# Spread tokens in SBUF instead of PSUM: a long convolution and a mixture of 4096 one-row experts on one core

## The chip, the cores and the metric

The kernel runs on one core of one Trainium2 chip. The metric is the device time of one execution in microseconds (us); lower is better. Five engines work side by side, each through its own queue of instructions in a fixed order, and wait for one another by semaphores: PE (matmul; PEld is its weight load), DVE (elementwise), ACT (activation functions and copies), POOL (here: it makes the descriptors of the indirect gathers and does some small arithmetic) and SP (issues the plain DMAs).

## The reference

Everything works on 2048 tokens of 448 channels. One half (A) is a long causal convolution per channel, the other (B) a layer of product-key experts:

```python
xn = _layernorm(x)
# A: short conv on k, times v, long conv by FFT, gate
kv = k_shift * v;  y = irfft(rfft(kv_pad) * rfft(k_pad))[:S] + kv * ssm_D;  A = xn * y
# B: 16 heads, two sets of 64 keys, best 2 of the 64x64 pairs
q1, q2 = halves of einsum("nd,dhc->nhc", xn, w_q)
s1, s2 = q1 @ k1.T, q2 @ k2.T          # two best of each, then two best sums
g = softmax(top_s);  ue, ve = u[top_e], v[top_e]
act = gelu(einsum("nd,nhkd->nhk", xn, ue))
B = einsum("nhk,nhk,nhkd->nd", g, act, ve)
out = x + A + B
```

B needs 2048 x 16 x 2 = 65536 gathered rows, each 448 numbers of `u` and 448 of `v` (3584 bytes): 235 MB, the bulk of the kernel's traffic.

## The kernel before

Tokens lie on the 128 partitions, 16 tiles T of them in `XA`. Scores are found with matmuls against weights folded from `w_q` and the keys, the best experts with MAX8 and FIND_INDEX8 on DVE; `place` turns the expert numbers into `idx` and the softmax weights into `gat`, spread so that one gather fetches, for 32 tokens, four experts each.

The expert work of a tile is cut into `NB` = 8 batches (128 in all, b = 8T + j). One batch is:

- **gather**: four indirect DMAs on POOL's queue (L586), each 128 rows of `u` and `v` side by side into one of the `ring`'s slots. The ring holds `RING` = 5 batches, so that the gathers of batch b + 5 wait until batch b has been used. A gather also waits for the landing of the sixth gather before it, and for a matmul on PE that the plan puts `LEAD` us ahead of it.
- **prod** (L619): one DVE multiplication of the four `u` slots (128 x 1792 numbers) with `xs`, the tile's tokens spread so that partition p holds the token of the row gathered there. Before, `xs` lies in PSUM (four of the eight banks), where `spread` (L607) writes it with four matmuls per tile.
- **sum** and **gelu** (L625, L627): four ACT copies with accumulation, then one small activation.
- **co** and **coef** (L633, L632): two small multiplications that make the matmul's weights `cc` from gelu, `gat` and a constant; on POOL up to batch 103, on DVE from `LATE` = 104 on.
- **val** (L638): four matmuls from `cc` and the `v` slots into `pv`, which gathers the tile's result in its own bank; `fold` (L673) takes it out.

The convolution (A) runs in between as matrix products in two parts: `conv_in` (L703 to L724), `spectrum` (L767 to L796), `inverse` (L814 to L839), `conv_out` (L858 to L881). In its elementwise steps DVE multiplies and adds pieces of `S`, which is in SBUF (L703, L704, L707 to L709, L795, L796), or a PSUM bank with SBUF (L788, L839).

All other matrix products share the remaining PSUM banks, three before: a product takes a slot with `acq`, and the instruction that reads it out last gives it back with `rel`.

The order of all this on each engine is made by a planner (`Plan.solve`): it goes through time, starts on each engine the ready operation with the smallest key, and knows durations, hops between engines and free banks. `RANK` shifts the keys of each group of operations along the kernel. The planner also fills planned gaps on PE between `val`s with idle matmuls (L1094), which write columns of `pv` that nobody reads.

Of the kernel before, what the change touches and what calls it, by code (L numbers as in the profile page):

```python
# [15 lines left out]
ALU = mybir.AluOpType  # L16
# [2 lines left out]
S, D, H, E = 2048, 448, 16, 64  # L19
NT = S // P  # L20
NB = 8
RING = 5


N = 2 * S
# [69 lines left out]
class Plan:  # L95
# [122 lines left out]
        "in1": (388.1, 396.9), "sp1": (396.9, 561.6), "out1": (561.6, 586.6)}  # L218
DMA_RATE = 0.421
OUTSTANDING = 6  # L220
LEAD = 2.0
RANK = {
# [6 lines left out]
    "SPlate@out1": (-46.5, -46.5, -46.5, -57.0), "SPwq": (0.0, 0.0, 45.5, 0.0), "SPx": (6.0, 6.0, 19.5, 22.0), "bad": (178.0, 100.0, 62.0, 46.5),  # L229
    "co": (-1740.0, 1197.0, -1227.0, -3082.0), "coef": (-33.5, -40.5, -46.0, 6.0), "ds": (22.0, -93.0, -157.5, -36.0),  # L230
    "es": (79.5, 106.0, 108.5, 109.0), "fin@out0": (-413.0, -296.5, -286.5, 40.5), "fin@out1": (0.5, -32.0, -27.5, -27.5),
    "flag": (-22.5, -47.5, -14.0, -53.0), "fold": (50.0, 36.5, 0.0, 0.0), "gat": (13.0, 13.0, 13.0, 9.0), "gate@out1": (6.5, 14.5, -60.5, -123.0),
    "gateG@out0": (83.0, -13.0, 54.5, 64.0), "gateG@out1": (-81.0, -64.5, -137.5, -144.0), "gather": (2080.5, 2339.0, 2195.5, 3324.0),
    "gelu": (164.5, 57.0, 133.0, 285.5), "hh@sp0": (8.0, -21.0, -25.0, -24.5), "hh@sp1": (123.5, 413.0, 124.0, 164.0),
    "idx": (-94.5, -44.0, 35.5, -83.0), "join": (-75.5, -75.5, -75.0, -66.0), "kv@in0": (-829.5, -476.5, -686.5, -690.5),
    "kv@in1": (85.0, 90.5, 112.5, 143.0), "landing": (36.0, 242.5, 1246.5, -266.5), "late@out1": (87.0, -40.5, -164.0, -260.0),
    "lateD@out1": (344.5, 342.0, 247.0, 196.0), "mi": (-280.5, -150.0, 455.5, 455.5), "mx": (-7077.5, -8642.5, -7977.0, -6331.5),
    "newton": (67.5, 142.0, 224.5, 283.5), "pk": (-14.5, -10.0, -32.0, -8.0), "place": (-628.5, -829.0, -301.5, -212.5),
# [6 lines left out]
    "stats": (1206.5, 960.0, 979.0, 837.5), "store": (43.0, 28.0, 12.5, 7.0), "storeD": (23.5, 22.0, 74.0, 52.5),  # L245
# [3 lines left out]
    "tw@sp1": (-23.5, -160.0, -53.5, -133.5), "val": (87.5, -236.5, 21.0, -42.0), "whi": (495.0, 545.0, 210.5, 67.0),  # L249
# [4 lines left out]
}  # L254
LATE = 104
DLAND = 1.2
# [17 lines left out]
def one_pass(ctx, tc, x, wq, kk, uv, kvh, cst1, cst2, fq, out, flag):  # L274
# [22 lines left out]
    ds = ap.tile([P, P], F32, name="ds")  # L297
    nw = ap.tile([P, 64], F32, name="nw")

    xs = pp.tile([P, 4, 512], F32, name="xs")  # L300
    pv = pp.tile([P, 512], F32, name="pv")
    bank = [pp.tile([P, 512], F32, name=f"bank{i}") for i in range(3)]

    ident, i4, rmask = c1[:, 0:P], c1[:, P:2 * P], c1[:, 2 * P:2 * P + 4]
    off8, one = c1[:, 2 * P + 4:2 * P + 12], c1[:, 2 * P + 12:]
# [35 lines left out]
    ws = [S1[:, D * i:D * i + D] for i in range(2)]  # L341

    pl = Plan()
    pl.pool("bank", 3)
    op = pl.op

    def load(dst, src, mb, w, key, nb=0.0, r=(), name=""):
# [46 lines left out]
    def tb(b):  # L394
        return T0 + PACE * min(b, TURN) + PACE2 * max(b - TURN, 0)
# [205 lines left out]
            landed.append(d)  # L601

    def spread(T):
        def f():
            for r in range(4):
                rs = slice(32 * r, 32 * r + 32)
                nc.tensor.matmul(xs[:, r, :D], i4[rs, :], XA[rs, T, :], start=True, stop=True, tile_position=(32 * r, 0))  # L607
        op("PE", 1.1, f, r=[("x", T), "c1"], w=["xs"], key=tb(NB * T) - 6.0, name="spread")

    def batch(T, j):  # L610
        b = NB * T + j
        k = tb(b)
        U = ring[:, b % RING, :, :D]
        aw = sm[:, 4 * (b % 4):4 * (b % 4) + 4]
        ge = sm[:, 16 + 4 * (b % 4):20 + 4 * (b % 4)]
        co = sm[:, 32 + 4 * (b % 4):36 + 4 * (b % 4)]
        u = [("U", b % RING, r) for r in range(4)]
        m = 4
        op("DVE", dve(m * D), lambda: nc.vector.tensor_mul(U[:, :m, :], U[:, :m, :], xs[:, :m, :D]), r=["xs"], w=u[:m], key=k, name="prod")  # L619
        for r in range(m, 4):  # L620
            op("DVE", 0.78, lambda r=r: nc.vector.scalar_tensor_tensor(U[:, r, :], xs[:, r, :D], 1.0, U[:, r, :], op0=ALU.mult, op1=ALU.mult,
                                                                      accum_out=aw[:, r:r + 1]),
               r=["xs"], w=[u[r], ("aw", b % 4, r)], key=k, name="dot")
        for r in range(m):
            op("ACT", 0.575, lambda r=r: nc.scalar.activation(U[:, r, :], U[:, r, :], AF.Copy, accum_out=aw[:, r:r + 1]),  # L625
               w=[u[r], ("aw", b % 4, r)], key=k, name="sum")
        op("ACT", 0.2, lambda: nc.scalar.activation(ge, aw, AF.Gelu_apprx_tanh), r=[("aw", b % 4, r) for r in range(4)], w=[("ge", b % 4)], key=k, name="gelu")  # L627

        ve, en, d0, d1 = (nc.vector, "DVE", 0.17, 0.3) if b >= LATE else (nc.gpsimd, "POOL", 0.22, 0.41)

        def coef():
            last_val(ve.tensor_mul(cc[b % 3], co[:, :, None].broadcast_to([P, 4, 32]), rep[:, None, :].broadcast_to([P, 4, 32])).ins, b - 3)  # L632
        op(en, d0, lambda: ve.tensor_mul(co, ge, gat[:, T % 8, :, j]), r=[("ge", b % 4), ("gat", T % 8, j // 2)], w=[("co", b % 4)], key=k - 40.0, name="co")  # L633
        op(en, d1, coef, r=[("co", b % 4), "c1"], w=[("cc", b % 3)], key=k - 40.0, name="coef")

        def val():
            for r in range(4):
                v = nc.tensor.matmul(pv[32 * r:32 * r + 32, :D], cc[b % 3][:, r, :], ring[:, b % RING, r, D:],  # L638
                                     start=(j == 0), stop=(j == NB - 1), tile_position=(0, 32 * r)).ins
                tc.declare_no_dep(v, group=GROUP + "s", reason="the coefficients come from all four gathered slots")  # L640
                if r < 3:
                    tc.add_to_no_dep_group(GROUP, v)
            vins[b] = v.name
        v = op("PE", 1.0, val, r=[("cc", b % 3)] + ([("pv", j - 1)] if j else []) + ([("pv", n) for n in more(T)] if j == NB - 1 else []), w=[("V", b % RING, r) for r in range(4)] + [("pv", j)] + (["pv"] if j == 0 else []), key=k, name="val")
        v.slot = j
# [511 lines left out]
```

## Time and profile before

| | |
|---|---|
| median of 3 runs | 918.38 us (917.74 to 920.84) |
| the profiled execution | 909.46 us, its span 907.5 us, granted clock 0.907 |
| PE / PEld busy | 750.7 / 474.3 us |
| DVE / ACT / POOL busy | 672.4 / 568.3 / 590.5 us |
| HBM read and written | 272.29 and 6.08 MB, 307 GB/s over the span |
| first and last gather start | 40.6 and 876.5 us |

Busy time is what an engine's instructions took. Waiting, issuing of DMAs and the pause between two gathers on POOL are not in it. In a row of groups stand the line, the engine, the operation, what it writes and reads, the count, then busy us and mean ns of one, then the idle time of that engine just before and what ended it.

### The profile page before, as it was taken

The numbers are of one execution on the slowest core, as the hardware profiler recorded it, in microseconds if no ns is written. First come the engines' busy times: TensorE is split into PE (matmuls) and PEld (weight loads), VectorE is DVE, ScalarE is ACT, GpSimd is POOL, SyncE is SP. The second block draws the span as 40 slices with busy tenths as digits, with TensorE's granted clock in tenths as the row PEclk, the third lists the DMA queues.
The fourth block names the chain that finished last, engine by engine and source line by source line (L and its number), as shares of the span: only waits on it lengthen the run. The fifth ranks groups of instructions, "written<-read, shape, count | busy, mean of one in ns | idle before, by whom it ended". The sixth has DMA issues, their size and how long they took to land.

```text
span 907.5 us, 15150 instructions
## 1 busy us (share of the span) xinstructions
PE 750.7 (83%) x4696; PEld 474.3 (52%) x4696; DVE 672.4 (74%) x1570; ACT 568.3 (63%) x1874; POOL 590.5 (65%) x740
## 2 busy tenths in 40 slices
PE   6978988898888888889798887788598897859776
PEld 2436655655565555556465555465343443436554
DVE  3667988797878877777878867658798897863553
ACT  2698664566556765566664576536698896864552
POOL 0157487877777766767677677747778776665640
PEclk9999999997999988989899889888989998986887
DMA  9998699888889898889899889988989999899975
GB/s 370 368 384 293 202 315 309 296 284 303 306 312 328 306 313 273 299 308 324 284 307 328 306 292 373 361 287 295 324 300 324 335 301 327 313 328 338 304 259 141
DMA packets 62586, 279.47 MB, mean 308 GB/s; under 512 B 14112, under 2 KB 23584, under 8 KB 62240
## 3 DMA queue, kind: packets, MB, share of 16 engines
q0 software_dynamic: 40960, 234.91, 74.4%
q1 hardware_dynamic: 21536, 43.49, 13.5%
q8 instruction: 39, 0.64, 0.3%
q14 instruction: 51, 0.42, 0.1%
HBM read 272.29 MB, written 6.08 MB: 307 GB/s over the span
## 4 chain that ended last, share of the span: by engine, by line
PE 42%; DVE 15%; issue 12%; POOL 10%; ACT 9%; DMA 8%; another core or an unknown queue 3%; DVEq 0%; POOLq 0%; SPq 0%; ACTq 0%
PE pv L638 9%; POOL ring L586 8%; DVE ring L619 4%; ACT ring L625 4%; DVE SC L486 4%; DMA ring<-in_uv_dram,idx 4%; PE bank L771 3%; PE bank L477 3%; PE bank L720 3%; PE bank L865 3%; PE pv L1094 3%; PE bank L478 3%; PE bank L479 3%; PE bank L814 2%
## 5 line engine op out<-in xcount | busy, mean ns | idle before, releaser
L586 POOL DMA_INDIRECT ring<-in_uv_dram,idx x512 | 505.4, 987 | 253.6 <-issue 91.9
L625 ACT ACTIVATE ring<-ring 128x448 f32<-128x448 f32 x512 | 288.3, 566 | 42.3 <-DVE ring L619 28.1
L619 DVE TENSOR_TENSOR ring<-ring,xs 128x1792 f32<-128x1792 f32 x128 | 256.8, 2013 | 36.1 <-DMA ring<-in_uv_dram,idx 28.0
L638 PE MATMUL pv<-ring,cc 128*32 128x448 f32 x1024 | 141.9, 622 | 49.1 <-POOL cc L632 24.6
L486 DVE MAX8 SC<-bank 128x8 f32<-128x64 f32 x512 | 118.4, 232 | 43.9 <-PE bank L481 12.2
L1094 PEld LDWEIGHTS pv<-c 128*128 128x128 f32 x596 | 82.1, 204 | 28.8 <-issue 27.8
L625 ACT ACTIVATION_READ_ACCUMULATOR ring<-ring 128x1 f32 x512 | 97.0, 189 | 0.0
L720 PE MATMUL bank<-c,S 128*64 128x132 f32 x896 | 71.6, 305 | 27.1 <-issue 7.5
L1094 PE MATMUL pv<-c 128*128 128x64 f32 x596 | 87.3, 287 | 2.5 <-issue 2.5
L477 PE MATMUL bank<-WR,xh 128*128 128x512 f32 x192 | 84.6, 441 | 4.9 <-issue 2.8
L720 PEld LDWEIGHTS bank<-c,S 128*64 128x64 f32 x896 | 56.2, 150 | 50.8 <-issue 22.6
L478 PE MATMUL bank<-WR,xh 128*128 128x512 f32 x192 | 77.0, 401 | 0.0
L479 PE MATMUL bank<-WR,xl 128*128 128x512 f32 x192 | 76.6, 399 | 0.0
L638 PEld LDWEIGHTS pv<-ring,cc 128*32 128x32 f32 x1024 | 21.6, 114 | 91.7 <-issue 37.2
L771 PE MATMUL bank<-x1b,S 128*128 128x336 f32 x132 | 53.0, 520 | 12.1 <-issue 4.6
L788 DVE TENSOR_TENSOR S<-bank,S 128x224 f32<-128x224 f32 (+1 forms) x66 | 40.6, 618 | 26.0 <-ACT S L782 12.1
L724 ACT ACTIVATE x1b<-bank 128x264 f32<-128x264 f32 x84 | 31.1, 387 | 45.5 <-PE bank L720 36.8
L703 DVE TENSOR_TENSOR S<-S 128x1024 f32<-128x1024 f32 x28 | 34.2, 1221 | 30.0 <-PE bank L720 11.4
L477 PEld LDWEIGHTS bank<-WR,xh 128*128 128x128 f32 x192 | 37.9, 197 | 29.6 <-issue 9.1
L493 DVE FIND_INDEX8 SC<-SC,bank 128x8 uint32<-128x256 f32 x128 | 52.5, 423 | 0.0
L632 POOL TENSOR_TENSOR cc<-sm,c 128x128 f32<-128x128 f32 x104 | 46.0, 443 | 2.1
L782 ACT ACTIVATE S<-bank 64x112 f32<-64x112 f32 x132 | 33.9, 256 | 18.2 <-PE bank L767 6.5
(142 smaller groups left out, 1102.8 us busy)
## 6 DMA issues: line engine op xcount, KB each, us to landing
R<-in_wq_dram SPq DMA_DIRECT2D x16, 896.0 KB
S<-in_kvh_dram SPq DMA_DIRECT2D x28, 400.0 KB
ring<-in_uv_dram,idx POOLq DMA_INDIRECT x512
S<-in_fq_dram SPq DMA_DIRECT2D x32, 128.0 KB
XA<-in_x_dram SPq DMA_DIRECT2D x2, 1344.0 KB
out_dram<-fo SPq DMA_DIRECT2D x12, 224.0 KB
x1b<-out_dram SPq DMA_DIRECT2D x9, 224.0 KB
out_dram<-XA SPq DMA_DIRECT2D x2, 840.0 KB
```

The source lines that it names most:

```text
L477: nc.tensor.matmul(o, xh[:, c, :], wh[:, c, ns], start=(c == 0), stop=False)
L478: nc.tensor.matmul(o, xh[:, c, :], wl[:, c, ns], start=False, stop=False)
L479: nc.tensor.matmul(o, xl[:, c, :], wh[:, c, ns], start=False, stop=False)
L486: nc.vector.max(mx[:, 8 * n + j, :] if safe else m2[:, m, 2 * j:2 * j + 8], bank[s.i][:, 64 * j:64 * j + 64])
L493: nc.vector.max_index(m4i[:, 2 * m + g, :], m2[:, m, 8 * g:8 * g + 8], bank[s.i][:, 256 * g:256 * g + 256])
L586: g = nc.gpsimd.indirect_dma_start(dst, None, uv, bass.IndirectOffsetOnAxis(ap=idx[:, T % 8, r, j:j + 1], axis=0)).ins
L619: op("DVE", dve(m * D), lambda: nc.vector.tensor_mul(U[:, :m, :], U[:, :m, :], xs[:, :m, :D]), r=["xs"], w=u[:m], key=k, name="prod")
L625: op("ACT", 0.575, lambda r=r: nc.scalar.activation(U[:, r, :], U[:, r, :], AF.Copy, accum_out=aw[:, r:r + 1]), w=[u[r], ("aw", b % 4, r)] ...
L638: v = nc.tensor.matmul(pv[32 * r:32 * r + 32, :D], cc[b % 3][:, r, :], ring[:, b % RING, r, D:], start=(j == 0), stop=(j == NB - 1), tile_ ...
L720: nc.tensor.matmul(o[64 * i:64 * i + 64, w * j:w * j + w], src, f1[:, i, :], start=True, stop=True, tile_position=(0, 64 * i))
L771: op("PE", 0.95 * n / 448 + 0.05, lambda t=t, sl=sl: nc.tensor.matmul(bank[sl.i][:, :n], fm, x1[p][:, :, q, t, :], start=True, stop=True), ...
L1094: nc.tensor.matmul(pv[:, D:], ident, c1[:, P:P + 512 - D], start=False, stop=False)
```

## The change

`xs` becomes an SBUF tile with two buffers, one for even and one for odd tiles. A spread matmul now writes an ordinary bank, and an ACT copy brings it to SBUF; there are four of each per tile. The product reads both operands from SBUF. The four PSUM banks that `xs` had go to the shared pool: seven instead of three. The SBUF that the two buffers take (14336 bytes per partition) is what the ring gives up: four batches instead of five. `LEAD` goes from 2.0 to 1.0, and all numbers in `RANK` are new, with seven points along the kernel instead of four.

```diff
-RING = 5
+RING = 4
...
-LEAD = 2.0
+LEAD = 1.0
 RANK = {
-    "DMAc1": (-1.0, 0.0, 8.0, 64.5), "DMAc2": (43.5, 4.0, 37.0, 128.5), ...
+    "DMAc1": (-28.0, -15.5, -74.0, -74.5, -52.5, -48.0, -73.5), ...
...
-    xs = pp.tile([P, 4, 512], F32, name="xs")
+    xs = ap.tile([P, 2, 4, D], F32, name="xs")
     pv = pp.tile([P, 512], F32, name="pv")
-    bank = [pp.tile([P, 512], F32, name=f"bank{i}") for i in range(3)]
+    bank = [pp.tile([P, 512], F32, name=f"bank{i}") for i in range(7)]
...
-    pl.pool("bank", 3)
+    pl.pool("bank", 7)
...
     def spread(T):
-        def f():
-            for r in range(4):
+        for r in range(4):
+            sl = Slot()
+
+            def f(r=r, sl=sl):
                 rs = slice(32 * r, 32 * r + 32)
-                nc.tensor.matmul(xs[:, r, :D], i4[rs, :], XA[rs, T, :], start=True, stop=True, tile_position=(32 * r, 0))
-        op("PE", 1.1, f, r=[("x", T), "c1"], w=["xs"], key=tb(NB * T) - 6.0, name="spread")
+                nc.tensor.matmul(bank[sl.i][:, :D], i4[rs, :], XA[rs, T, :], start=True, stop=True, tile_position=(32 * r, 0))
+            k = tb(NB * T) - 12.0
+            op("PE", 0.27, f, r=[("x", T), "c1"], w=[("sp", r)], key=k, acq=("bank", sl), name="spread")
+            op("ACT", 0.54, lambda r=r, sl=sl: nc.scalar.activation(xs[:, T % 2, r, :], bank[sl.i][:, :D], AF.Copy), r=[("sp", r)], w=[("xs", T % 2, r)],
+               key=k, rel=("bank", sl), name="xs")
...
-        op("DVE", dve(m * D), lambda: nc.vector.tensor_mul(U[:, :m, :], U[:, :m, :], xs[:, :m, :D]), r=["xs"], w=u[:m], key=k, name="prod")
+        op("DVE", dve(m * D), lambda: nc.vector.tensor_mul(U[:, :m, :], U[:, :m, :], xs[:, T % 2, :m, :]), r=[("xs", T % 2, r) for r in range(4)], w=u[:m], key=k, name="prod")
```

Three places show what the new order does. In these rows `bank0` and so on are PSUM slots, `cc0` to `cc2` the coefficients in turn, L477 to L481 (L494 to L498 after) the score products, L767 and L814 (L832 after) convolution products.

PE at the spread of tile 6, before: one write into `xs`, after the `val` of batch 46 (the tile's first batch is 48).

```order
L480 MATMUL bank2_88<-WR_93,xh_95 128x512
L481 MATMUL bank2_88<-WR_93,xl_96 128x512
L638 MATMUL pv_85<-ring_66,cc1_75 32x448 x4
L607 MATMUL xs_84<-XA_65,c1_67 128x448 x4
L767 MATMUL bank0_86<-R1_94,S1_72 128x224
L638 MATMUL pv_85<-ring_66,cc2_76 32x448 x4
L767 MATMUL bank1_87<-R1_94,S1_72 128x224
```

PE at the spread of tile 6 after: two of its four matmuls, each into a bank of its own, after the `val` of batch 30.

```order
L656 MATMUL pv_85<-ring_66,cc2_76 32x448 x4
L832 MATMUL bank3_89<-S1_72,c2_68 128x112 x4
L656 MATMUL pv_85<-ring_66,cc0_74 32x448 x4
L832 MATMUL bank3_89<-S1_72,c2_68 128x112 x4
L626 MATMUL bank1_87<-XA_65,c1_67 128x448
L626 MATMUL bank5_91<-XA_65,c1_67 128x448
L494 MATMUL bank6_92<-WR_97,xh_99 128x512
```

The spread moved two tiles ahead of its use; it no longer holds one fixed place in PSUM until the tile is done, but each part needs a free slot and an ACT copy that frees it.

ACT around batch 47, the last of tile 5, before: the sums (L625) and the gelu (L627) of one batch after another, with convolution copies (L782) and the fold (L673).

```order
L627 ACTIVATE sm_77<-sm_77 128x4
L625 ACTIVATE ring_66,sm_77<-ring_66 128x448 x4
L627 ACTIVATE sm_77<-sm_77 128x4
L782 ACTIVATE S1_72<-bank0_86 64x112 x4
L673 ACTIVATE fo_69<-pv_85,mv_78 128x448
```

ACT at the same place after: the four copies into `xs` (L629) for tile 7 come in one piece behind the sums (L643) of batch 46 and ahead of those of batch 47.

```order
L643 ACTIVATE ring_66,sm_77<-ring_66 128x448 x4
L645 ACTIVATE sm_77<-sm_77 128x4
L853 ACTIVATE R1_98<-bank4_90,c2_68 128x28x4 x2
L629 ACTIVATE xs_84<-bank6_92 128x448
L629 ACTIVATE xs_84<-bank1_87 128x448
L629 ACTIVATE xs_84<-bank5_91 128x448
L629 ACTIVATE xs_84<-bank2_88 128x448
L643 ACTIVATE ring_66,sm_77<-ring_66 128x448 x4
L645 ACTIVATE sm_77<-sm_77 128x4
```

ACT has four more instructions per tile; they stand nine batches ahead of the first product that reads them, batch 56.

POOL around batch 40, before: gathers (L586) with co (L633) and coef (L632) woven in; when the coef of batch 40 (the L632 that writes `cc1`) comes, 18 gathers beyond the 160 of the batches up to 39 have been issued.

```order
L586 DMA ring_66<-in_uv_dram,idx_70 128x896 x7
L633 TENSOR_TENSOR sm_77<-sm_77,gat_71 128x4
L586 DMA ring_66<-in_uv_dram,idx_70 128x896
L632 TENSOR_TENSOR cc1_75<-sm_77,c1_67 128x128
L586 DMA ring_66<-in_uv_dram,idx_70 128x896
L633 TENSOR_TENSOR sm_77<-sm_77,gat_71 128x4
L586 DMA ring_66<-in_uv_dram,idx_70 128x896
L632 TENSOR_TENSOR cc2_76<-sm_77,c1_67 128x128
```

POOL around batch 40 after: the same instructions, L603, L651 and L650, with 12 gathers beyond the 160 at the coef of batch 40 (`cc1`).

```order
L603 DMA ring_66<-in_uv_dram,idx_70 128x896 x5
L651 TENSOR_TENSOR sm_77<-sm_77,gat_71 128x4
L650 TENSOR_TENSOR cc0_74<-sm_77,c1_67 128x128
L651 TENSOR_TENSOR sm_77<-sm_77,gat_71 128x4
L650 TENSOR_TENSOR cc1_75<-sm_77,c1_67 128x128
L603 DMA ring_66<-in_uv_dram,idx_70 128x896 x2
L651 TENSOR_TENSOR sm_77<-sm_77,gat_71 128x4
L603 DMA ring_66<-in_uv_dram,idx_70 128x896
L650 TENSOR_TENSOR cc2_76<-sm_77,c1_67 128x128
```

POOL's work is the same 512 gathers, 104 co and 104 coef; its gathers run up to one batch and a half less ahead of the coefficients.

More of the change, by code (lines that the diff above doesn't have):

```diff
@@ L220 @@
 OUTSTANDING = 6
-LEAD = 2.0
+LEAD = 1.0
 RANK = {
[6 rows of a table removed]
[L229 to L238, printed above, removed]
[6 rows of a table removed]
-    "stats": (1206.5, 960.0, 979.0, 837.5), "store": (43.0, 28.0, 12.5, 7.0), "storeD": (23.5, 22.0, 74.0, 52.5),
[3 rows of a table removed]
-    "tw@sp1": (-23.5, -160.0, -53.5, -133.5), "val": (87.5, -236.5, 21.0, -42.0), "whi": (495.0, 545.0, 210.5, 67.0),
[4 rows of a table removed]
[10 rows of a table added]
+    "SPx": (15.0, 15.0, 15.0, 15.0, 11.0, 15.0, 15.0), "bad": (38.5, 47.0, 35.5, 26.0, 69.5, 47.5, 29.0),
[3 rows of a table added]
+    "flag": (6.0, -5.0, -5.0, -5.0, -5.0, -18.0, -5.0), "fold": (-1.0, -18.5, -44.0, -58.5, 8.5, 14.0, 7.5),
[20 rows of a table added]
+    "stats": (1100.5, 1019.5, 922.5, 949.5, 972.5, 929.5, 942.5), "store": (-4.5, -12.0, -9.0, -1.5, -3.0, -4.0, -4.0),
[5 rows of a table added]
+    "val": (96.5, -364.5, -547.5, -311.5, 22.5, -332.5, 206.5), "whi": (43.0, 58.5, 20.5, 3.5, -28.5, -19.5, -19.5),
[6 rows of a table added]
 }
@@ L618, in batch @@
         m = 4
[L619 to L623, printed above, removed]
+        op("DVE", dve(m * D), lambda: nc.vector.tensor_mul(U[:, :m, :], U[:, :m, :], xs[:, T % 2, :m, :]), r=[("xs", T % 2, r) for r in range(4)], w=u[:m], key=k, name="prod")
         for r in range(m):
```

63 rows, old and new, of the table RANK are left out of this document.

## The prediction

> **What bounds the kernel now.** I read the page's head, then the stretches, then POOL's waits, its timeline against DVE's, and the groups.
>
> ```profile
> span 907.5 us, 15150 instructions
> PE 750.7 (83%) x4696; PEld 474.3 (52%) x4696; DVE 672.4 (74%) x1570; ACT 568.3 (63%) x1874; POOL 590.5 (65%) x740
> ...
> 0.00:77.00 77.00, 60.61 (x324) 31.24 (x328) 43.49 (x156) 49.18 (x156) 21.96 (x32) 0.96 0.94 367
> 77.00:877.00 800.00, 670.63 (x4266) 428.41 (x4258) 616.82 (x1397) 510.93 (x1696) 568.04 (x709) 0.91 0.89 308
> 877.00:907.50 30.50, 19.49 (x110) 14.63 (x110) 12.10 (x19) 8.16 (x24) 0.47 (x1) 0.69 0.51 147
> ```
>
> The page's 65% for POOL hides its pauses. In the timeline a gather begins 0.30 us after a gather and 0.16 us after a small multiplication:
>
> ```profile
> 636.26 0.96 POOL L586 DMA_INDIRECT ring<-in_uv_dram,idx  x1
> 637.24 0.41 POOL L632 TENSOR_TENSOR cc<-sm,c 128x128 f32<-128x128 f32 x1
> 637.81 1.90 POOL L586 DMA_INDIRECT ring<-in_uv_dram,idx  x1 [0.16 <-issue]
> 640.02 0.95 POOL L586 DMA_INDIRECT ring<-in_uv_dram,idx  x1 [0.30 <-PE bank L720]
> ...
> 77.00:877.00 800.00, 484.81 (x491) 0.91 0.89 308
> ...
> 77.00:877.00 800.00, 6.07 (x21) 45.18 (x102) 0.91 0.89 308
> ```
>
> The last two rows are the stretch for the gathers (L586) and for coef (L632: DVE's, then POOL's): 491 gathers, 102 coefs on POOL, and a co (L633) to each. So about 204 gathers follow a multiplication and 287 a gather: 204 x 0.16 + 287 x 0.30 = 119 us of pauses. POOL's time is then 568 + 119 = 687 of 800 us, 86%: it is as full as PE (671 us, which includes idle matmuls). 113 us are real waiting:
>
> ```profile
> POOL ring L586 <- issue: 86.4, 330, 1.2
> POOL sm L633 <- ACT sm L627: 23.4, 19, 3.3
> POOL ring L586 <- PE bank L720: 15.9, 21, 4.0
> POOL ring L586 <- PE pv L638: 13.9, 16, 2.0
> POOL ring L586 <- remote: 11.7, 13, 2.0
> ```
>
> The first row is the pauses; the rest, and a tail of smaller rows, are spread thin. No engine has a large reserve that the others could lean on, and POOL has 14%.
>
> **The product's second operand.** This term decides. The gather that took 1.90 us above, where 0.95 is usual, began inside a DVE instruction that reads two SBUF tensors:
>
> ```profile
> 637.64 1.22 DVE L703 TENSOR_TENSOR S<-S 128x1024 f32<-128x1024 f32 x1
> ...
> L586 POOL DMA_INDIRECT ring<-in_uv_dram,idx x512: 940/948/1978, 40.6 to 876.5; - x171
> ...
> 106.83 1.81 POOL L586 DMA_INDIRECT ring<-in_uv_dram,idx  x1 [0.30 <-issue]
> ...
> 106.60 1.22 DVE L703 TENSOR_TENSOR S<-S 128x1024 f32<-128x1024 f32 x1
> ```
>
> L703 ended at 638.86, the gather at 639.71: 0.85 later. At 106.83 L703 ended at 107.82 and the gather at 108.64: 0.82 later. All 13 gathers that began inside L703 with more than 0.25 us of it left did this (these two are the first and the last). A gather thus needs about 0.13 us at its start that it cannot have while such an instruction runs; then it goes on. The product of today does not do that:
>
> ```profile
> 57.40 0.94 POOL L586 DMA_INDIRECT ring<-in_uv_dram,idx  x1 [6.04 <-ACT gat L562]
> 876.52 0.95 POOL L586 DMA_INDIRECT ring<-in_uv_dram,idx  x1 [0.30 <-issue]
> ...
> 55.99 2.02 DVE L619 TENSOR_TENSOR ring<-ring,xs 128x1792 f32<-128x1792 f32 x1
> 876.28 2.02 DVE L619 TENSOR_TENSOR ring<-ring,xs 128x1792 f32<-128x1792 f32 x1 [3.10 <-DMA ring<-in_uv_dram,idx]
> ```
>
> These are the first and the last of 163 gathers that began inside a product; the longest took 1.0 us. The one difference that fits is that `xs` is in PSUM. Co and coef behave alike: coef on POOL spans 398/409/1457 ns, and its long ones (such as the first row here) began inside S<-S instructions.
>
> ```profile
> 625.15 1.42 POOL L632 TENSOR_TENSOR cc<-sm,c 128x128 f32<-128x128 f32 x1
> ...
> L632 POOL TENSOR_TENSOR cc<-sm,c x104: 398/409/1457, 64.2 to 744.0; 128x128 f32<-128x128 f32 x104
> ```
>
> After the change all 128 products are of the holding kind, and each is longer than L703.
>
> [...]
>
> **The parts of the change and their cost.**
>
> *Hold by the product.* I laid the two timelines over one another: in 121 of 128 products some gather, co or coef starts. Counting only the first start in each product, since POOL is in order, and the product's remaining time less 0.13 us for a gather, the sum is 160 us, 1.25 per product. A check from spacing: a product lasts 2.01 us, and a busy POOL starts something about every 0.95 + 0.30 us, so the first start comes 0.6 us into it and waits 2.01 - 0.6 - 0.1 = 1.3. Best case, each product begins right behind a gather's start: 2.01 - 1.25 - 0.13 = 0.63, or 81 us. Worst case, a start right behind each product's: 2.01 - 0.13, or 241 us. I take 155 for the 123 products of the middle stretch.
>
> *The product itself* costs about the same:
>
> ```profile
> L619 DVE TENSOR_TENSOR ring<-ring,xs x128: 1998/2012/2022, 56.0 to 882.4; 128x1792 f32<-128x1792 f32 x128
> L703 DVE TENSOR_TENSOR S<-S x28: 1205/1224/1226, 81.3 to 642.8; 128x1024 f32<-128x1024 f32 x28
> L707 DVE TENSOR_TENSOR S<-S x21: 673/691/694, 491.8 to 644.2; 128x512 f32<-128x512 f32 x21
> ```
>
> From 512 to 1024 numbers takes 533 ns, 1.04 each, with 158 fixed; 1792 give 2.02 us, 11 ns more than now and 1.4 us over 128. DVE has room for it. [...]
>
> *ACT copies.* 64 copies, priced by a copy of that shape:
>
> ```profile
> L418 ACT ACTIVATE S<-bank x16: 519/530/544, 13.5 to 66.4; 128x448 f32<-128x448 f32 x16
> ```
>
> That is 34 us on an engine with 511 of 800 us busy, nine batches ahead of use: nothing on the path. If that cover failed, each tile would pay 4 x 0.53 = 2.1 us behind the sums, 34 us in all. The wait that goes, a product for the spread, was 3.3 us in 3 cases; next late there is the landing of the gathers (28.0 us in 18 cases).
>
> *Seven banks.* What PE or its weight loads waited for an eviction by ACT or DVE:
>
> ```profile
> PE bank L767 <- ACT ring L625: 8.2, 3, 4.1
> PE bank L865 <- ACT S L860: 6.4, 5, 3.0
> PEld bank L767 <- ACT ring L625: 12.1, 6, 4.3
> PEld bank L865 <- ACT S L860: 10.8, 7, 3.8
> PEld bank L720 <- ACT ring L625: 10.6, 15, 1.9
> PEld bank L720 <- ACT x1b L724: 8.6, 6, 2.9
> ```
>
> These are 57 us, smaller rows bring perhaps as much; part of it is data that was late, not a bank. Bounds 0 to about 60 us on PE. It reaches the end only through POOL's waits for PE (the bank and pv rows above), so I let it shorten those and count it there. The new `LEAD` ties a gather to a matmul that ends 1 us later than before, which works against it. The plan now has 354 idle matmuls instead of 298:
>
> ```profile
> L1094 PE MATMUL pv<-c 128*128 128x64 f32 x596 | 87.3, 287 | 2.5 <-issue 2.5
> ```
>
> At 87.3/298 = 0.29 us each, 56 more are 16 us of PE, in its planned gaps and hidden while PE waits; without that cover they would take 16 us from the banks' gain.
>
> *Ring of four.* A slot's life from its first gather's start to the end of its `val` is 27.5 us on average (first and last row of the two lists: 40.6 and 876.5 for L586, 56.0 and 882.4 for L619), and 4.7 us pass until it is gathered into again: 32.2 us, five periods of 6.4. For the last batch, with nothing in its way, 882.4 - 877.5 = 4.9 us lie between the end of its last gather and its product; the mean of all is 9.9. So about 5 us are reserve, and four slots can be served every (32.2 - 5)/4 = 6.8 us. With POOL at (687 + 155)/123 = 6.8 us per batch the ring just keeps up, without reserve: cost 0 in the middle, up to 60 us if nothing of the 5 can be given up.
>
> **The sum.** Middle stretch: POOL 687 + 155 = 842 us without any wait. That alone is more than the 800 of now. Of the 113 us waiting, much vanishes, since engines that POOL waited for get ahead of it; what remains lies between 0 and 113, and I take a quarter, 28, near the low end because the banks help there. 870 + 77.0 before + 30.5 behind = 977.5 us span, 979.5 with the 2.0 us outside it. The profiled execution (909.46) stands 8.9 us under the median of the runs (918.38), so I add that: 988 us, +7.6%.
>
> **Rivals.**
> - *The ring binds too.* For: POOL's run-ahead shrinks from 18 to 12 gathers at batch 40, and co waits for ACT already (23.4 us). Against: the 5 us reserve. All 113 us of waiting stay or more: 842 + 113 + 107.5 + 2 + 9 = 1073 us.
> - *Only co and coef are held, gathers are not.* 25 + 40 us of products remain over them in the timelines; half of 65 disappears in the waits: 918 + 33 = 951, less up to 30 from the banks: 921 to 951. Against: the 13 of 13. [...]
> - *The hold does not come, and the banks pay.* The rows with L703 would owe their length to something else, such as that instruction's overlapping window. Then POOL stays at 86%, and PE's 57 us of waits for evictions fall: half reaches the end, 918 - 28 = 890 us. It decides if gathers inside products stay at 0.95 us. Against: a plain pair of operands (L795) holds a gather too, to 0.83 us behind its end:
>
> ```profile
> 786.48 1.23 POOL L586 DMA_INDIRECT ring<-in_uv_dram,idx  x1 [0.30 <-DMA ring<-in_uv_dram,idx]
> ...
> 786.38 0.50 DVE L795 TENSOR_TENSOR Y<-S 64x336 f32<-64x336 f32 x1
> ```
>
> - *Nothing moves*: hold and banks cancel, which needs about 40 us from the banks beyond my sum: 915 to 921.
>
> **How the numbers follow.** Runs of this kernel spread over 0.3%, 918 to 921, so 0.3% is what a measurement can tell from no change. The hold as summed: 0.72, with its own range 938 (hold 110 us, a fifth of the waiting stays) to 1045 (three quarters of the waiting stay). Ring binding as well, 1045 to 1073 and beyond: 0.12. Only co and coef: 0.06, mostly slower. Banks pay, 890: 0.07. Nothing: 0.03. That makes slower 0.88, within 0.3% 0.04, faster 0.08. The range 938 to 1060 leaves out nearly all of the last three and the upper half of the ring case, 0.2 in all.
>
> **What the changed profile would show.** Right: gathers that begin inside a product end 0.82 us behind it, their mean rises from 0.99 to about 1.25 us and POOL's busy time to about 740; coef rises to about 0.6 us; the product stays at 2.02; POOL's waits shrink while waits for cc and for landings grow; PE's clock and busy time change little. Wrong: gathers at 0.95 us inside products; or POOL's waits gone and the time still up, which would be the ring (gathers waiting for `val`); or DVE's product itself longer than 2.1 us, held by POOL in turn.

## The result, and the profile after

The changed kernel took 1035.2 us (median of 5 runs, 1028.8 to 1042.0); the kernel before, run between them, took 920.8 us. The ratio is 1.127, with a 95% interval of 1.122 to 1.131: slower by about an eighth. The prediction was 988 us, in a range of 938 to 1060. The profiled execution took 1028.8 us, at a granted clock of 0.857.

The head of the page, and the three stretches, cut again at 77 us and some 30 us ahead of the end:

```profile
span 1026.7 us, 15388 instructions
PE 835.4 (81%) x4808; PEld 529.2 (52%) x4808; DVE 680.2 (66%) x1570; ACT 600.0 (58%) x1938; POOL 745.9 (73%) x740
...
0.00:77.00 77.00, 56.25 (x275) 25.91 (x275) 38.59 (x149) 41.23 (x122) 17.37 (x24) 0.96 0.89 339
77.00:996.00 919.00, 756.34 (x4418) 487.38 (x4410) 627.71 (x1401) 548.25 (x1786) 722.97 (x712) 0.86 0.82 269
996.00:1026.70 30.70, 22.81 (x125) 15.88 (x124) 13.92 (x22) 10.51 (x33) 5.61 (x5) 0.67 0.67 196
```

The columns behind the length are PE, PEld, DVE, ACT, POOL, then granted clock, DMA share and GB/s. POOL made the same 740 instructions as before and was busy for 745.9 us in place of 590.5. All of the 119 us by which the span grew lie in the middle stretch, 919 us in place of 800, and POOL's busy time there rose by 155.

The timeline of after shows why. A row is start, length, engine, line, what it writes and reads; "x2" is two instructions in a row.

```profile
74.06 4.29 DVE L641 TENSOR_TENSOR ring<-ring,xs 128x1792 f32<-128x1792 f32 x2
...
76.63 2.58 POOL L603 DMA_INDIRECT ring<-in_uv_dram,idx  x1 [0.16 <-issue]
...
129.95 2.02 DVE L641 TENSOR_TENSOR ring<-ring,xs 128x1792 f32<-128x1792 f32 x1
130.89 1.34 POOL L650 TENSOR_TENSOR cc<-sm,c 128x128 f32<-128x128 f32 x1
...
1000.64 2.03 DVE L641 TENSOR_TENSOR ring<-ring,xs 128x1792 f32<-128x1792 f32 x1 [1.61 <-DMA ring<-in_uv_dram,idx]
1002.21 1.28 POOL L603 DMA_INDIRECT ring<-in_uv_dram,idx  x1 [0.96 <-issue]
```

The products end at 78.35 and 1002.67, the gathers that began inside them at 79.21 and 1003.49: 0.86 and 0.82 us later. These are the first and the last of 89 gathers that began inside a product with more than 0.25 us of it left. 83 of them ended 0.81 to 0.86 us behind it; the other six had begun within 0.03 us of the product's start and took 0.95 to 0.96 us, as if there were no product. The 89 took 2.14 us on average. The coef at 130.89 ends 0.26 us behind its product; all 16 such coefs end 0.25 to 0.26 us behind their product, all 18 such co's 0.06 to 0.07 us behind theirs. Before, 137 gathers began inside a product like that and took 0.95.

The groups of the page (count, then busy us and mean ns, then the idle time just before them and what ended most of it):

```profile
L603 POOL DMA_INDIRECT ring<-in_uv_dram,idx x512 | 609.9, 1191 | 236.6 <-issue 94.5
L641 DVE TENSOR_TENSOR ring<-ring,xs 128x1792 f32<-128x1792 f32 x128 | 261.0, 2041 | 148.6 <-DMA ring<-in_uv_dram,idx 137.0
...
L656 PE MATMUL pv<-ring,cc 128*32 128x448 f32 x1024 | 149.0, 663 | 110.5 <-POOL cc L650 97.7
...
L650 POOL TENSOR_TENSOR cc<-sm,c 128x128 f32<-128x128 f32 x104 | 69.4, 668 | 3.1
L651 POOL TENSOR_TENSOR sm<-sm,gat 128x4 f32<-128x4 f32 x104 | 48.6, 468 | 6.7 <-ACT SC L552 2.0
```

The gather's mean is 1191 ns, coef's 668. The waits of after (us in total, times, longest):

```profile
DVE ring L641 <- DMA ring<-in_uv_dram,idx: 137.0, 60, 6.0
PEld pv L656 <- POOL cc L650: 123.6, 67, 5.8
PE pv L656 <- POOL cc L650: 97.7, 54, 5.7
...
POOL ring L603 <- issue: 94.5, 358, 1.0
POOL ring L603 <- ACT idx L579: 50.4, 1, 50.4
...
POOL ring L603 <- PE pv L656: 25.8, 22, 2.4
...
POOL ring L603 <- PE bank L738: 11.8, 13, 2.6
```

DVE now waits for gathers to land (137.0 us; before 28.0), and PE for the coefficients that POOL is late with (97.7 us; before 24.6). POOL itself waits for little: its largest row is the pause between gathers, and the 50.4 us are the one wait for the first `idx`, at the start. The chain of waits says the same; the first row is of before, the second of after.

```profile
PE 42%; DVE 15%; issue 12%; POOL 10%; ACT 9%; DMA 8%; another core or an unknown queue 3%; DVEq 0%; POOLq 0%; SPq 0%; ACTq 0%
```

```profile
PE 32%; POOL 31%; issue 16%; DMA 10%; DVE 7%; ACT 2%; another core or an unknown queue 1%; POOLq 0%; SPq 0%; DVEq 0%
```

POOL's share of the chain has gone from 10% to 31%, and with "issue", three quarters of which stands ahead of POOL's instructions, it carries the most.

### The profile page after: what moved, and what is told of

Same layout as the page of the kernel before. It is cut to its first block, busy times and chain, and to the rows that moved or that the text cites. A ratio compares the mean times of both kernels' runs of the same rounds, so it can differ in the third digit from the quotient of the medians.

```text
span 1026.7 us, 15388 instructions
## 1 busy us (share of the span) xinstructions
PE 835.4 (81%) x4808; PEld 529.2 (52%) x4808; DVE 680.2 (66%) x1570; ACT 600.0 (58%) x1938; POOL 745.9 (73%) x740
## 4 chain that ended last, share of the span: by engine, by line
PE 32%; POOL 31%; issue 16%; DMA 10%; DVE 7%; ACT 2%; another core or an unknown queue 1%; POOLq 0%; SPq 0%; DVEq 0%
POOL ring L603 23%; DMA ring<-in_uv_dram,idx 8%; PE pv L656 6%; POOL cc L650 4%; PE bank L738 3%; POOL sm L651 3%; PE pv L1112 3%; PE bank L432 3%; PE bank L494 3%; PE bank L883 2%; DMA R<-in_wq_dram 2%; PE bank L495 2%; PE bank L496 2%; DVE SC L503 2%; DVE ring L641 2%
## 5 line engine op out<-in xcount | busy, mean ns | idle before, releaser
L603 POOL DMA_INDIRECT ring<-in_uv_dram,idx x512 | 609.9, 1191 | 236.6 <-issue 94.5
L641 DVE TENSOR_TENSOR ring<-ring,xs 128x1792 f32<-128x1792 f32 x128 | 261.0, 2041 | 148.6 <-DMA ring<-in_uv_dram,idx 137.0
L643 ACT ACTIVATE ring<-ring 128x448 f32<-128x448 f32 x512 | 289.0, 568 | 97.0 <-DVE ring L641 94.7
L656 PE MATMUL pv<-ring,cc 128*32 128x448 f32 x1024 | 149.0, 663 | 110.5 <-POOL cc L650 97.7
L1112 PEld LDWEIGHTS pv<-c 128*128 128x128 f32 x708 | 105.2, 221 | 35.5 <-issue 33.9
L1112 PE MATMUL pv<-c 128*128 128x64 f32 x708 | 111.3, 305 | 0.0
L643 ACT ACTIVATION_READ_ACCUMULATOR ring<-ring 128x1 f32 x512 | 97.7, 191 | 0.0
L738 PE MATMUL bank<-c,S 128*64 128x132 f32 x896 | 82.5, 342 | 15.5 <-DVE SC L510 5.7
L494 PE MATMUL bank<-WR,xh 128*128 128x512 f32 x192 | 87.5, 456 | 2.2 <-DVE SC L510 1.1
L738 PEld LDWEIGHTS bank<-c,S 128*64 128x64 f32 x896 | 66.4, 172 | 39.7 <-issue 15.3
L495 PE MATMUL bank<-WR,xh 128*128 128x512 f32 x192 | 80.2, 418 | 0.0
L650 POOL TENSOR_TENSOR cc<-sm,c 128x128 f32<-128x128 f32 x104 | 69.4, 668 | 3.1
L651 POOL TENSOR_TENSOR sm<-sm,gat 128x4 f32<-128x4 f32 x104 | 48.6, 468 | 6.7 <-ACT SC L552 2.0
L494 PEld LDWEIGHTS bank<-WR,xh 128*128 128x128 f32 x192 | 39.8, 207 | 26.1 <-issue 6.4
L806 DVE TENSOR_TENSOR S<-bank,S 128x224 f32<-128x224 f32 (+1 forms) x66 | 40.7, 618 | 15.3 <-PE bank L789 4.9
```

What stands on the lines that cost most here:

```text
L494: nc.tensor.matmul(o, xh[:, c, :], wh[:, c, ns], start=(c == 0), stop=False)
L495: nc.tensor.matmul(o, xh[:, c, :], wl[:, c, ns], start=False, stop=False)
L603: g = nc.gpsimd.indirect_dma_start(dst, None, uv, bass.IndirectOffsetOnAxis(ap=idx[:, T % 8, r, j:j + 1], axis=0)).ins
L738: nc.tensor.matmul(o[64 * i:64 * i + 64, w * j:w * j + w], src, f1[:, i, :], start=True, stop=True, tile_position=(0, 64 * i))
L1112: nc.tensor.matmul(pv[:, D:], ident, c1[:, P:P + 512 - D], start=False, stop=False)
```

## The experiments

The theory: a product that reads two SBUF tensors keeps POOL from starting a gather, co or coef until it ends, and that is nearly all of the loss. The rivals: the ring of four binds; the new order and `LEAD` are worse by themselves; the ACT copies and the spread through the banks are in the way. Each ratio is to the kernel before on the same chip. The chips differ: the kernel before takes 840 us on two of those used and about 920 on the third and in the comparison above, with granted clocks of about 0.945 and 0.90. So ratios are compared within a chip.

**The changed kernel again, on a chip where the kernel before takes 841 us.** No edit.

> The changed kernel unchanged, on the chip of the next three, as their base. Where the kernel before runs at 920 us the ratio is 1.12 to 1.14. Hold theory: POOL's own time sets the pace (842 us of it in the middle stretch), which no faster chip shortens; where the kernel before runs at 840 us, the changed one still needs 980 to 1030 us, a ratio near 1.2. Clock rival (the granted clock carries the loss): the ratio stays at 1.13 there.

Measured: 1025.8 us, ratio 1.218 (1.210 to 1.227), POOL busy 752.2 us. The kernel before gains 80 us from the faster chip, the changed kernel 9. That is what a kernel paced by POOL would do. But its granted clock didn't rise on this chip either (0.852 here, 0.857 above), so this run alone doesn't part POOL's work from PE's clock. That POOL sets the pace rests on the middle stretch of the profile above: POOL's work (723 us) and pauses (126) fill 849 of its 919 us.

**Only the operand, in the kernel before.** The ring of five, the three banks and the order stay (but for a few instructions of POOL and ACT near the start); the product reads its second operand from a constant in SBUF.

```diff
-nc.vector.tensor_mul(U[:, :m, :], U[:, :m, :], xs[:, :m, :D])
+nc.vector.tensor_mul(U[:, :m, :], U[:, :m, :], c2[:, None, :D].broadcast_to([P, m, D]))
```

> The kernel before (ring of five, three slots, old order) with one edit: the product multiplies by a constant block of the SBUF tables instead of by the spread tokens in PSUM. The spread is still written and not read, so the expert part has other numbers. Hold theory: POOL busy rises from 590 to about 745 us and the time to 1000 us (975 to 1035). Ring or order rival: 915 to 930 us, since ring, banks and order are those of before.

Measured: 987.5 us, ratio 1.177 (1.168 to 1.186). Its page:

```profile
span 989.5 us, 15138 instructions
PE 776.4 (78%) x4696; PEld 494.4 (50%) x4696; DVE 676.3 (68%) x1570; ACT 569.9 (58%) x1874; POOL 763.5 (77%) x740
...
L586 POOL DMA_INDIRECT ring<-in_uv_dram,idx x512 | 619.2, 1209 | 188.1 <-issue 86.3
L619 DVE TENSOR_TENSOR ring<-ring,c 128x1792 f32<-128x1792 f32 x128 | 259.4, 2033 | 85.4 <-DMA ring<-in_uv_dram,idx 83.2
```

One operand moved to SBUF, nothing else, costs 147 us; the product no longer waits for the spread, which can't explain a loss. Gathers and POOL's busy time are like those of the changed kernel. The product is hardly slower (2033 ns in place of 2012), so it isn't DVE that pays. This run names the main cause.

**Only the operand, the other way: the changed kernel without the hold.** The product becomes a reduction of the same size that reads one SBUF tensor; the order is the same instruction for instruction.

```diff
-nc.vector.tensor_mul(U[:, :m, :], U[:, :m, :], xs[:, T % 2, :m, :])
+nc.vector.reduce_sum(nw[:, 56:60], U[:, :m, :], axis=mybir.AxisListType.X)
```

> The changed kernel, same order on every engine, with the product replaced by a DVE reduction of the same 128 x 1792 numbers, which reads one SBUF tensor; the multiplication by the tokens is left out, the spread and its copies are made. Hold theory: gathers inside the reduction take 0.95 us, POOL busy falls from 746 to about 600 us, and the time comes to 0.97 to 1.05 of the kernel before. Ring or order rival: with POOL freed the time stays over 1.08 of the kernel before, and gathers wait for matmuls and coefficients instead.

Measured: 901.3 us, ratio 1.072 (1.066 to 1.077), on the chip on which the changed kernel took 1025.8.

```profile
PE 777.6 (86%) x4808; PEld 493.7 (55%) x4808; DVE 672.7 (75%) x1570; ACT 598.3 (67%) x1938; POOL 591.4 (66%) x740
...
L603 POOL DMA_INDIRECT ring<-in_uv_dram,idx x512 | 505.9, 988 | 259.2 <-issue 84.1
L641 DVE TENSOR_REDUCE nw<-ring 128x4 f32<-128x1792 f32 x128 | 257.8, 2014 | 108.2 <-DMA ring<-in_uv_dram,idx 99.4
```

The reduction takes as long on DVE as the product did (2014 ns), ACT's sums still wait for it (110.6 us, 94.7 for the product in the profile above), and still the gather is back at 988 ns and POOL at 591.4 us. 124.5 of the 184.8 us between the changed kernel and the one before on this chip went with the hold; PE's granted clock rose with it, from 0.852 to 0.916, and what that gave is in the 124.5. The other 60 us remain: 1.072 lies above the 1.05 of the theory and below the 1.08 of the rival. So the hold is two thirds of the loss on this chip, not nearly all of it, and something else in the change costs as well.

**The same work in shorter pieces.** The product in two instructions, and in four.

```diff
-nc.vector.tensor_mul(U[:, :m, :], U[:, :m, :], xs[:, T % 2, :m, :])
+[nc.vector.tensor_mul(U[:, i:i + 2, :], U[:, i:i + 2, :], xs[:, T % 2, i:i + 2, :]) for i in range(0, 4, 2)]
```

> The changed kernel, same order, each product made by two instructions of half the size; the result is the reference's. DVE pays 128 x 0.16 = 20 us more. Hold theory: a waiting gather gets in between the halves, so the hold per product falls from 1.25 to about 0.5 us: POOL busy 640 to 670 us, and 60 to 90 us less than the unchanged one on this chip. If the loss were the ring, the order or DVE's time: the same time or up to 20 us more.

> As the last, with four instructions of 128 x 448. DVE pays 128 x 3 x 0.16 = 61 us more. Hold theory: hold per product 0.15 to 0.3 us, POOL busy 610 to 640 us, and the time 80 to 115 us under the unchanged one on this chip, a little less than the reduction gains, since DVE is 60 us longer. If POOL is not what the hold delays: no gain and up to 60 us more.

Measured, two pieces: 959.3 us, ratio 1.142 (1.137 to 1.147).

```profile
L603 POOL DMA_INDIRECT ring<-in_uv_dram,idx x512 | 572.0, 1117 | 238.9 <-issue 73.4
L641 DVE TENSOR_TENSOR ring<-ring,xs 128x896 f32<-128x896 f32 x256 | 279.5, 1115 | 100.1 <-DMA ring<-in_uv_dram,idx 95.2
```

Four pieces: 917.2 us, ratio 1.090 (1.084 to 1.095).

```profile
L603 POOL DMA_INDIRECT ring<-in_uv_dram,idx x512 | 545.6, 1066 | 228.3 <-issue 55.6
L641 DVE TENSOR_TENSOR ring<-ring,xs 128x448 f32<-128x448 f32 x512 | 307.7, 648 | 63.6 <-DMA ring<-in_uv_dram,idx 60.4
```

DVE does the same multiplications and pays 47 us more for the starts (307.7 against 261.0), and the kernel gets faster by 109 us. One piece, two, four, none: 1026, 959, 917, 901 us, with POOL busy for 752, 683, 652 and 591 us. The length of the single instruction is what counts: a gather waits until the instruction over it ends, and can start between two pieces. With four pieces, 126 of the 136 gathers that begin inside a piece with more than 0.25 us left end 0.81 to 0.86 us behind that piece. POOL stays busier than was expected for the pieces, since a gather that comes inside a short piece still waits to its end (a mean of 1066 ns with four, 988 with none). The pieces change one thing more: ACT can begin its sums behind the first piece, and its waits for L641, 94.7 us in the profile above, fall to 40.3 and 24.8. What that gave isn't parted from the hold here, so this series alone doesn't price the hold.

**Six slots, and then the product with its second operand in PSUM.** The first kernel gives one of the seven banks away, the second uses that bank for a constant operand. Both are planned anew, with the same `RANK`; PE, ACT and POOL run the same instructions in the same order in the two.

```diff
-bank = [... for i in range(7)];  pl.pool("bank", 7)
+bank = [... for i in range(6)];  pl.pool("bank", 6)
```

```diff
+xd = pp.tile([P, 512], F32, name="xd")     # filled with 1.0 once
-nc.vector.tensor_mul(U[:, :m, :], U[:, :m, :], xs[:, T % 2, :m, :])
+nc.vector.tensor_mul(U[:, :m, :], U[:, :m, :], xd[:, None, :D].broadcast_to([P, m, D]))
```

> The changed kernel with six slots in the shared PSUM pool instead of seven, all else the same; the eighth bank stays empty. It is the control for the next run. Hold theory (products that read two SBUF tensors keep POOL from starting): the number of banks hardly matters, 1020 to 1050 us, POOL busy 735 to 755 us. Bank rival (the seven slots carry the time): 10 us or more above the changed kernel's 1035 us.

> The control of six slots with one edit: the product multiplies by a constant bank in PSUM, which is set to one at the start, instead of by the token copies in SBUF. Spread matmuls and ACT copies are still made and read by nobody, so the expert part has other numbers; shapes and counts are the same. Hold theory: gathers that begin inside a product take 0.95 us again, POOL busy falls from 746 to about 590 us, the time to 920 us (900 to 945). Ring or order rival (four batches or the new order cost the time): above 990 us, POOL's busy time down but its waits for matmuls up by the same amount. Only-arithmetic rival (gathers are not held): POOL busy falls by at most 65 us.

Measured: 1154.9 us, ratio 1.376 (1.368 to 1.383), with POOL busy for 740.9 us; and 1049.6 us, ratio 1.250 (1.241 to 1.258), with POOL busy for 582.9 us. Both levels missed, on the side that the rivals had named: one slot fewer with the `RANK` of seven gives an order that is 129 us worse than the changed kernel on an equally fast chip (its gathers wait for one `val` up to 40.7 us). Slots and order changed together here, so this kernel doesn't price the number of banks. The difference within the pair does say something: 105 us back when the second operand comes from PSUM.

**The ring of four in the kernel before**, planned anew with the old `RANK`.

```diff
-RING = 5
+RING = 4
```

> The kernel before with a ring of four batches instead of five, planned anew with the old rank table. Hold theory: the ring costs little while POOL has its 14% of reserve, 918 to 940 us. Ring rival: 960 us or more, with gathers that wait for the matmuls which free a slot.

Measured: 920.7 us, ratio 1.097 (1.090 to 1.103), POOL busy 592.2 us. This is more than the theory allowed, whose 918 to 940 us were meant for a chip at 920 us, a ratio of up to 1.02. But the order is new as well, and the six slots have shown how much a new order can carry, so this run can't price the ring. The next pair can.

**The ring with the order fixed.** The reduction kernel without the ACT copies and without the `xs` tile, which leaves SBUF for a fifth slot; once with four batches in the ring (`RB` = 4), once with five.

```diff
-dst = ring[:, b % RING, r, :];  last_val(g, b - RING)
+dst = ring[:, b % RB, r, :];    last_val(g, b - RB)
```

> The kernel with the reduction in place of the product (multiplication by the tokens left out), and now without the 64 ACT copies and their SBUF tile too; order on every engine as planned for the changed kernel. It is the control for the next run. Copies rival (34 us of ACT cost time): 10 us or more under the reduction with copies (901 us where the kernel before takes 841). Hold and ring theories: within 8 us of it.

> As the last, with five batches of ring memory in place of four, in the SBUF that the copies' tile frees; the order on every engine stays that planned for four, only the wait of a gather for its slot is one batch looser. Ring theory (of the 7% that stays without the hold, the missing slot is the larger part): 20 to 45 us less than the last, gathers hardly wait for the products that free a slot. Order theory (the planned order, its pace marks and its later start are what stays): 0 to 10 us less.

Measured, on the chip where the kernel before takes 922 us: 951.7 us, ratio 1.039 (1.030 to 1.048), and 937.7 us, ratio 1.018 (1.007 to 1.028). The fifth slot is worth 14 us, between the two expectations, and the intervals just miss one another. The ring is a small part. It also shows that without copies and with five slots the new order is still not ahead of the old one. Whether the copies cost time can't be read from the first of the two: the kernel with copies ran on the faster chip.

**`LEAD` back at 2.0**, in the reduction kernel with its copies and four slots; the order on every engine stays, and each gather is tied to a matmul that the plan ends 1 us earlier.

> The kernel with the reduction (copies made, ring of four), with LEAD at 2.0 as in the kernel before; the order is the same, each gather is tied to a matmul that the plan ends 1 us earlier. Pace theory: gathers waited for matmuls, so 10 to 30 us less than 901. Ring or order theory: within 8 us of it.

Measured: 965.3 us, ratio 1.049 (1.037 to 1.062). Beside the kernel without copies at `LEAD` 1.0 on this chip (951.7) that is no gain. Copies and `LEAD` differ at once, and the kernel with copies at `LEAD` 1.0 ran on the faster chip, so neither theory is decided.

**The same remedy in the kernel before.** There L703, two SBUF operands and 1.22 us, holds 13 gathers; it is cut into two halves.

```diff
-nc.vector.tensor_mul(taps, win, st[...])
+for a in range(0, BC, 2):
+    nc.vector.tensor_mul(taps[:, a:a + 2], <win, two of four>, st[:, a:a + 2, ...])
```

> The kernel before, same order, with the 1024-number multiplication of the convolution's taps (L703, two SBUF tensors, 28 times) made in two halves; the result is the reference's. DVE pays 28 x 0.16 = 4.4 us. Hold theory: the 13 held gathers and some coefs wait half as long, about 8 us less of POOL's time; if half of it reaches the end, 0.5% less than the kernel before (0.990 to 1.000). If POOL's reserve of 14% hides it all: 1.000 to 1.005.

Measured: 918.6 us against 922.1, ratio 0.996 (0.991 to 1.001).

```profile
PE 759.7 (83%) x4696; PEld 484.5 (53%) x4696; DVE 675.6 (73%) x1598; ACT 566.2 (61%) x1874; POOL 581.3 (63%) x740
...
L586 POOL DMA_INDIRECT ring<-in_uv_dram,idx x512 | 498.6, 974 | 273.2 <-issue 97.0
```

POOL is relieved by 9 us (590.5 before) and the gather by 13 ns each. The ratio lies in the range of the hold theory, but its interval holds 1.000 too, so the two expectations aren't parted. No version was clearly faster than the kernel before.

## Why the prediction was right, and where it was off

*The hold* was the term that decided, and it came as reckoned: 155 us were taken for the middle stretch, and POOL's busy time there rose by 155 with three instructions more. Laid over one another again, the timelines of after give 162 us over all products by the same count that gave 160 before; that 155 met 155 to the microsecond is luck, since the order in which POOL's starts meet the products is new. Gathers end 0.82 us behind the product as said, POOL is busy for 746 us ("about 740"), coef takes 0.67 us ("about 0.6"), a gather 1.19 ("about 1.25"). Against the rival "only co and coef", 921 to 951 us, stand 83 gathers of 89; the other six began within 0.03 us of the product's start. With the reduction, which reads one SBUF tensor, the gather's mean was 988 ns (987 before). Why a second operand in SBUF holds POOL isn't shown.

*The product itself*: 11 ns more were reckoned, 29 came (2041 in place of 2012), 4 us in all. Its longest took 2.75 us. With the constant in SBUF it was 2033.

*POOL's remaining waits* are the term that was mis-sized, and most of the miss against the profiled time. The prediction kept a quarter of 113, 28 us. In after the gaps on POOL in the middle stretch, less 0.30 us behind a gather, 0.16 behind a multiplication and 0.03 ahead of one, sum to 70 us, and the pauses to 126 in place of 119: 42 and 7 us more, and 1026.7 less the predicted span of 977.5 is 49.2. The reason given, "the banks help there", did not carry. After the pauses and the start, the largest row is the wait for `val`, 25.8 us in place of 13.9, and the pair with four slots (first row) and five (second row) shows what most of that row is:

```profile
POOL ring L603 <- PE pv L656: 31.9, 24, 4.2
POOL ring L603 <- PE pv L656: 6.5, 9, 1.4
```

With the fifth slot 25 us of this row go, and the time falls by 14. So a part of what remained is the missing slot, which the prediction put at nothing. On chips where the kernel before takes about 840 us, the same count gives 25 us in the old kernel with the operand alone in SBUF, 63 in the changed kernel and 98 in the changed kernel without the hold. With the hold, then, the changed kernel waits some 38 us more than the old order does; how that divides between order, slots and copies was not measured. The kernel before left no trace on such a chip, so how much of its own waiting the hold hid isn't known: the quarter was a guess.

*Seven banks*, 0 to 60 us of gain, brought none that can be seen: POOL's rows for PE's `bank` did not go away (11.8 us for L738 beside 15.9 for L720 before), and without the hold the changed kernel is behind the old one on both kinds of chip (1.07, and 1.04 without copies). What the seven banks would give with the old order is open: no run had that pair alone.

*The ring* was said to keep up without reserve, at 0 to 60 us; its price is about 14, measured without the hold. Together with the hold it could be more, which wasn't run.

*The start* was taken as unchanged, 77.0 us. POOL's first gather comes at 51.5 us in place of 40.6 and its 41st at 144.9 in place of 118.8. In the first 60 us of after, PE waits longer for the loads of `wq`:

```profile
PE bank L432 <- DMA R<-in_wq_dram: 14.9, 3, 10.8
```

Before, that row (L415) had 8.5 us with 6.2 as the longest. Since the stretch was cut at 77 us, the loss stands in the middle: 24 of POOL's instructions lie ahead of the cut, before 32. What this costs at the end can be read from traces of the chip at 922 us. With the old order (the run with L703 halved) the 41st gather starts at 120.5 us and the span is 920.8. With the new order, without hold and copies and with five slots, it starts at 142.1 and the span is 936.4: 21.6 us late there and 15.6 at the end, so behind the 41st gather this order is no slower than the old one. With four slots it is 21.0 us late there and 29.0 at the end. These are single executions, and on the faster chip the 60 us that remain can't be divided like this. So the late start and the slot account for what stays without the hold and the copies on this chip; that the loads of `wq` cause the late start is argued, not shown.

*ACT copies hidden*: nothing speaks against it (the product's row for them is absent from the waits, and ACT is busy 60%), but the run that took them away alone was on another chip than the one with them, so it isn't shown.

*PE's clock and busy time change little*: wrong. PE was busy for 835 us in place of 751, at 0.857 in place of 0.907, with 112 matmuls more in 4808. This had no part in the sum, since POOL set the pace.

## What to carry to other kernels

Where POOL issues indirect gathers, look on DVE for instructions with two SBUF operands that run beside them: here each held POOL's next start until it ended (83 of 89 gathers ended 0.81 to 0.86 us behind the product), so price them by what is left of them when POOL starts under them, against POOL's true reserve (its pauses counted in). Leave one operand in PSUM (105 us less here, with six slots), or cut the instruction into pieces (109 us less with four); moving an operand to SBUF to free PSUM can cost more than it brings (147 us here by itself). An order made for given numbers of slots can be bad with others (129 us here): change one thing with the order kept, or the order's own loss hides the effect.

## What the hardware showed that was not expected

The granted clock was lower where POOL held the others up. With the order the same and only DVE's product changed, it was 0.852 with the hold and 0.916 without (changed kernel, profiled executions on one chip), and PE was busy for 834 and 778 us with the same 4808 matmuls: the two differ by factors of 1.07 and 1.08. So PE's busy time is no fixed load: with a change elsewhere the same work on PE looked bigger. Why less clock was granted isn't shown.

POOL seems to hold DVE a little in turn: the product with two SBUF operands has a mean of 2033 to 2067 ns in these kernels, with PSUM or one operand 2012 to 2018. In the changed kernel all 22 products over 2.04 us began while an instruction of POOL was running or within 0.03 us of one's start; so did 84 of the shorter ones.
